# Four tiles in place of one four-bank tile, and a new written order of all work, in a scan followed by a gated feed-forward kernel

## The chip, the cores and the metric

The kernel runs on one core of one Trainium2 chip. The metric is the device time of one execution in microseconds. TensorE is called PE (its weight loads PEld), VectorE DVE, ScalarE ACT, GpSimd POOL and SyncE SP; SP issues nearly all transfers.

## The reference

Inputs are x (4 batches, 8 heads, 768 positions, 32 wide), a (a decay per position), B and C (16 wide), and three weight matrices. Everything is float32. First comes a linear recurrence over the positions, in chunks of 32:

```
L = exp(cum_i - cum_j) * causal;  M = (C B^T) * L
y = M x + (C state) * exp(cum)
state = exp(sum la) * state + sum_j B_j x_j exp(cum_last - cum_j)
```

Then y, as 3072 tokens of 256, goes through a gated layer: `(sigmoid(y @ w_gate) * (y @ w_val)) @ w_out`, with a hidden width of 1536.

## The kernel before

**Work.** The 768 positions are six chunks of 128, numbered 0 to 5. A chunk's scan is a set of small matmuls on 64x64 or 32x128 pieces: `scan` (L494) writes the four-bank PSUM tile pcb and the local states, DVE's `decays` (L458) makes the decays by four scans (L464), `weigh` (L518) multiplies and adds up y with matmuls at L593 and L534. Each chunk gives 512 tokens, a block of the gated layer. Products are made in about float32 by splitting each operand into a high and a low fp32r part and adding three matmuls.

**Blocks 0 to 3** (`gate`, `value`, `proj`). For each f of 0 to 11 the products pg and pv (six matmuls each, L871; block 0 uses whole float32 weights for its first ones, L850, L862, L901) go to one of three PSUM banks. ACT takes the sigmoid of pg (L800), DVE multiplies pv with it (L824, the value gate), ACT and POOL split the result (L828, L830). `proj` then makes the output in two halves, in three steps of four f's each.

**Blocks 4 and 5 together** (`unit`, L1011). Their gate and value products for one weight i are a 2x2 block product, made with seven products in place of eight. A unit has two accumulators x and z, each a bank. Units with i % 3 == 2 (2, 5, 8, 11) take banks 2 and 3 of the tile acc, the others take banks of the pools of three and one. Between the products, `kept` copies a bank (L1042, ACT or DVE) and `summed` adds a bank to a copy (L1050, DVE); `gated` and `hidden` make the sigmoid (L1061, L1064) and the gated product (L1074, L936) and split it (L1088, L936). `paired_proj` (L1098) adds block 4's output into banks 0 and 1 of acc (L1110). `last_proj` makes block 5's output at the end. The unit's third operand, sums of weights, is made on POOL and DVE, stored to DRAM (w_s) and loaded again (s, L964), which may start when block 3's last value product (value3_11) is done.

**Weights.** w0 to w11 are the gate and value weights (even i gate, odd i value, two f's each), w12 to w17 the output weights. After its load each is converted on DVE, ACT, DVE, ACT, POOL (`split_w`, L365 to L385) and, most of them, split (`part_w`, L400, L402).

**Order.** The program writes out each engine's instructions in one fixed order, and the framework puts a semaphore wait wherever an instruction touches a tile that another engine touched. The order is found by a planner (`run`, L215), which acts before the program exists. Each task (`gate1_3`, `decays2`, `w5`) is a chain of steps with an engine, an assumed cost, needs and makes. Over and over it finds the step that could begin first, and takes, among the steps of that engine that could begin within 0.1 us of it, the one whose task has the lowest due time. Due times stand in DUES or, where it has no entry, come from the code at the end: decays2 has 85.0, value1_f has 77 + 2.74 f, weigh5 183, value3_11 206.5. It looks at the 400 tasks of lowest due time only.

Of the kernel before, what the change touches and what calls it, by code (L numbers as in the profile page):

```python
# [8 lines left out]
F32 = mybir.dt.float32  # L9
# [80 lines left out]
def tile_ssd_then_gated_ffn(  # L90
# [39 lines left out]
    ps_cb = ctx.enter_context(tc.tile_pool(name="ps_cb", bufs=1, space=PSUM))  # L130
# [84 lines left out]
    def run():  # L215
# [10 lines left out]
        spare = {"y": [0.0], "cb": [0.0], "cx": [], "cz": [], "o": [0.0] * 4}  # L226

        tasks.sort(key=lambda t: t[:2])
        while tasks:
            ready_ones = []  # L230
            for n, (_, _, (eng, cost, needs, makes, port, buffers, take, give), ready, gen, name) in enumerate(tasks[:400]):
                if any(k not in made for k in needs) or any(m > len(spare[k]) for k, m in buffers.items()):
                    continue
                banks = sum(k == "bank" for k, _ in take)
                some = len(take) - banks
                if some > len(rooms) or any(t is None for t in turns[-3 : len(turns) - 3 + banks]):
                    continue
                ready = max([ready] + turns[-3 : len(turns) - 3 + banks] + [t for t, _ in rooms[:some]])
                for k, m in buffers.items():
                    ready = max([ready] + spare[k][: max(m, 0)])  # L240

                def begin(e):
                    s = max([free[e], ready] + [made[k][0] for k in needs if made[k][1] != e or e == "sp"])
                    return max(s, port_free[0]) if e == "pool" or (e == "dve" and port) else s

                if not isinstance(eng, str):
                    cost, eng = min(zip(cost, eng), key=lambda ce: begin(ce[1]) + ce[0] + SPARE * (ce[1] == "dve"))
                ready_ones.append((begin(eng), eng, n, cost))
# [116 lines left out]
    def split_w(i):  # L365

        yield step("dve", DVE_1, [("raw", i)], port=True)
        raw = raws.pop(i)  # L370
        lw, hw = raw[:, :, :, 0], raw[:, :, :, 1]
        nc.vector.tensor_scalar(
            out=hw.bitcast(F32), in0=hw.bitcast(F32), scalar1=-W_MAX, scalar2=W_MAX, op0=ALU.max, op1=ALU.min
        )
        yield step("act", ACT_SB, [("t", i - 2)])
        t = wk.tile([P, 2, 2 * P], F32, tag="ut", name=f"wt{i}")
        nc.scalar.activation(t, hw.bitcast(F32), AF.Prelu, scale=2.0**-112, alpha=2.0**32)
        yield step("dve", DVE_1, [], [("t", i)], port=True)
        nc.vector.tensor_scalar(
            out=hw, in0=t.bitcast(U32), scalar1=3, scalar2=None, op0=ALU.logical_shift_left  # L380
        )
        yield step("act", ACT_SB, [("raw", i)])
        nc.scalar.activation(lw.bitcast(I32), lw, AF.Copy, scale=2.0**-29)  # L383
        yield step("pool", 1.08, [], [("whole", i)])
        nc.gpsimd.tensor_tensor(out=lw.bitcast(I32), in0=hw.bitcast(I32), in1=lw.bitcast(I32), op=ALU.add)  # L385
        whole[i] = lw.bitcast(F32)
        halves[i] = hw.bitcast(F32), lw.bitcast(F32)

    halves = {}

# [225 lines left out]
    class FirstUnit:  # L616
# [64 lines left out]
        def result(self):  # L681
# [6 lines left out]
            yield step("pe", 0.75, [("xn", b), ("first", 0, b - 1), ("bdec", 0, b)], [("y", 0, b)] + [("y", 0)] * (b == NB - 1), banks=1, y=1)  # L688
# [146 lines left out]
    def needs_of(k, f, j):  # L835
        xs = [("xp", i) for i in range(2)] if k == 0 and not thin(k, f) else [("x", k, i) for i in range(NB)] if k == 0 else [("x", k)]
        return [("whole" if thin(k, f) else "w", f // 2 * 2 + j)] + xs + ([("pv", k, f - 1)] if f else []) + ([("proj", k - 1)] if f > 2 else [])
# [44 lines left out]
    def proj(k, m):  # L882
# [3 lines left out]
        for n, f in enumerate(fs):  # L886
            start, stop = n == 0, n == NF - 1
            if n % 4 == 0:
# [3 lines left out]
                if n == 0:  # L892
                    needs.append(("gv", k))
                yield step(
# [116 lines left out]
    def unit(i):  # L1011
# [5 lines left out]
        if kind == 2:  # L1017
            x, z = (got["acc"][:, n] for n in (2, 3))
# [35 lines left out]
    def gated(j, n):  # L1054
# [3 lines left out]
        if n == 2:  # L1058
            yield step("act", ACT_MM, [("unit", i)], [("sig", j, n)], take=[("g", ("c", i, n))], **drop)
# [3 lines left out]
        yield step("act", ACT_SB, [("c", i, n)], [("sig", j, n)])  # L1063
        nc.scalar.activation(got["c", i, n], got["c", i, n], AF.Sigmoid)  # L1064

    def hidden(j, n):
# [3 lines left out]
        if n == 2:  # L1070
            drop = ({"give": [("bank", ("X", i))]}, {"give": [("bank", ("X", i))]}, {"cx": -1})[i % 3]
            yield step("dve", DVE_MM, [("unit", i), ("sig", j, n)], **drop)
# [3 lines left out]
        else:  # L1076
            eng = yield step(("dve", "pool"), (DVE_SB, POOL_SB), [("c", i, n), ("sig", j, n)], port=True, give=[("g", ("c", i - 1, n))])
# [14 lines left out]
    def accumulators():  # L1092

        yield step("none", 0.0, [("S", NCH - 1)], [("acc",)], cb=1)
        got["acc"] = ps_cb.tile([P, NQ, 512], F32, tag="pcb", name="acc")
        yield step("none", 0.0, cx=-1, cz=-1)

    def paired_proj(j):  # L1098

        for m in range(NK):  # L1100
# [5 lines left out]
            for n in range(2):  # L1106
                hi, lo = (wo[j][:, n, p, ms] for p in range(2))
                hh, hl = (hs[SA, 2 * j + n][:, p] for p in range(2))
                for q, (a, b) in enumerate(((hi, hh), (hi, hl), (lo, hh))):
                    nc.tensor.matmul(  # L1110
                        got["acc"][:, m], a, b, start=(j == 0 and n == 0 and q == 0), stop=(q == 2), skip_group_check=True
                    )

    def paired_out(m):

        yield step("none", 0.0, [("po", SA, m, NF // 2 - 1)])
        yield from turned_out(SA, m, got["acc"][:, m], {}, "act" if m else "sp")
# [99 lines left out]
    def loads_of(c):  # L1217
        block = [("gv", 0)] if c == 2 else []

        def some(key, n, transfer, size, needs, fns):  # L1220
# [3 lines left out]
            **some("a", 2, 2.75, 64, [("y", max(c - 2, 0)), ("a_z",)], lambda: load_a(c)),  # L1224
            **some("bq", 2 * NB, 0.18, 128, [("bt", c - 1)], lambda: load_rows("bq", c, Bm, 1)),
            **some("cq", 2 * NB, 0.18, 128, [("ct", c - 1), ("tp", NB - 1)], lambda: load_rows("cq", c, Cm, 1)),
            f"bn{c}": load(1, 3.2, 4096, [("bdec", c - 2)] + block, [("bn", c)], lambda: load_tokens("bn", c, b4, N, 2)),
# [4 lines left out]
    def initial():  # L1232

        made = [(k, c) for k in ("bt", "ct", "cd", "bdec") for c in (-1, 0)]
        made += [("y", -1), ("t", -2), ("t", -1), ("first", 0, -1), ("inter", 0, -2), ("inter", 0, -1)]
# [14 lines left out]
    for b in range(NB):  # L1250
        named[f"b{b}"] = load(2, 1.5, 1024, [], [("bc", b)], lambda b=b: load_bc(b))
        named[f"x{b}"] = load(1, 0.9, 1024, [], [("xn", b)], lambda b=b: load_x(b))
# [110 lines left out]
```

## Time and profile before

| | us |
|---|---|
| median of 3 runs | 372.23 (371.36 to 374.55) |
| the profiled execution | 372.0 |
| its span, first to last instruction | 370.0 |
| PE busy | 350.0 (95%) |
| POOL, DVE, ACT busy | 248.6, 178.1, 158.5 |
| PE's granted clock, mean | 0.986 of full speed |

Shares are of the span. A matmul counts from its start to a modelled end, and successive matmuls overlap. Times in the rows are from the start of the span.

### The profile page before, as it was taken

How to read it: one execution, taken by the hardware profiler on the slowest of the kernel's cores; microseconds unless marked ns; L12 is line 12 of the kernel's file. 1: busy time of each engine (PE TensorE's matmuls, PEld its weight loads, DVE VectorE, ACT ScalarE, POOL GpSimd, SP SyncE). 2: the span in 40 equal slices, each digit the busy share in tenths (PEclk: the TensorE clock that was granted, in tenths of full speed). 3: DMA queues.
4: the chain of work that ended last, by engine and by line, in shares of the span. 5: the costliest groups of instructions: out<-in, count | busy, mean ns of one | idle time of the engine just before them, and what ended most of it. 6: DMA issues, size and time to landing. Idle time of an engine off the chain costs nothing.

```text
span 370.0 us, 7942 instructions
## 1 busy us (share of the span) xinstructions
PE 350.0 (95%) x3138; PEld 266.1 (72%) x3138; DVE 178.1 (48%) x295; ACT 158.5 (43%) x290; POOL 248.6 (67%) x247
## 2 busy tenths in 40 slices
PE   8989999999979899999999999969998899989896
PEld 3674487567857688888887888758885677757685
DVE  5977686655477554464640536500143425424221
ACT  2667396316733510364412444332075456537200
POOL 3556286684987584489975588749758598947700
PEclk9999999999989999999999999978999999999999
DMA  7987999483934872376344601131354233300013
GB/s 146 191 260 253 218 233 212 90 82 55 177 57 51 124 160 57 105 131 137 103 55 112 113 15 57 47 128 57 89 171 126 70 114 115 113 0 3 0 31 83
DMA packets 100247, 40.15 MB, mean 109 GB/s; under 512 B 88754, under 2 KB 91826, under 8 KB 99570
## 3 DMA queue, kind: packets, MB, share of 16 engines
q1 hardware_dynamic: 97906, 39.39, 47.9%
q8 instruction: 24, 0.39, 0.5%
q10 hardware_dynamic: 2304, 0.26, 0.5%
q14 instruction: 13, 0.11, 0.1%
HBM read 30.00 MB, written 9.63 MB: 107 GB/s over the span
## 4 chain that ended last, share of the span: by engine, by line
PE 76%; DMA 6%; SPq 6%; DVE 5%; issue 4%; ACT 1%; ACTq 1%; DVEq 0%
PE pg L871 15%; PE pv L871 15%; PE po L905 5%; PE acc L1009 5%; PE po L907 5%; PE po L906 5%; PE acc L1110 5%; PE po L901 5%; PE ux L1009 5%; DMA wr<-in_moe_w_gate_dram 4%; PE uz L1009 3%; DVE c L1050 3%; SPq L321 2%; PE pcb L593 2%; DMA wr<-in_moe_w_val_dram 2%
## 5 line engine op out<-in xcount | busy, mean ns | idle before, releaser
L830 POOL TENSOR_TENSOR h<-g,h 128x512 fp32r<-128x512 f32 x38 | 55.7, 1471 | 17.8 <-ACT h L828 17.6
L871 PE MATMUL pg<-xh,w 128*128 128x512 f32 x168 | 59.4, 394 | 2.7 <-DVE g L824 2.3
L871 PE MATMUL pv<-xh,w 128*128 128x512 f32 x168 | 59.6, 395 | 0.0
L824 DVE TENSOR_TENSOR g<-pv,g 128x512 f32<-128x512 f32 x38 | 26.0, 687 | 38.9 <-PE pv L871 35.9
L800 ACT ACTIVATE g<-pg 128x512 f32<-128x512 f32 x48 | 28.8, 600 | 30.7 <-PE pg L871 25.7
L828 ACT CAST h<-g 128x512 fp32r<-128x512 f32 x38 | 23.6, 621 | 39.9 <-DVE g L824 39.6
L871 PEld LDWEIGHTS pg<-xh,w 128*128 128x128 f32 x168 | 31.7, 189 | 10.7 <-DVE g L824 2.8
L936 POOL TENSOR_TENSOR h<-c,h 128x512 fp32r<-128x512 f32 x24 | 30.8, 1298 | 10.0 <-ACT h L1088 10.0
L871 PEld LDWEIGHTS pv<-xh,w 128*128 128x128 f32 x168 | 32.1, 191 | 6.9
L464 DVE TENSOR_TENSOR_SCAN ab<-ab,delta 128x512 f32<-128x512 f32 x20 | 32.7, 1662 | 2.2 <-DMA ab<-a_z 2.2
L871 PE MATMUL pv<-xl,w 128*128 128x512 f32 x84 | 33.2, 395 | 0.0
L871 PE MATMUL pg<-xl,w 128*128 128x512 f32 x84 | 33.0, 392 | 0.0
L905 PE MATMUL po<-h,w 128*128 128x512 f32 x76 | 31.9, 420 | 0.0
L936 POOL TENSOR_TENSOR c<-c,c 128x512 f32<-128x512 f32 x18 | 23.1, 1297 | 11.1 <-DVE c L1050 6.7
L907 PE MATMUL po<-h,w 128*128 128x512 f32 x76 | 30.6, 402 | 0.0
L906 PE MATMUL po<-h,w 128*128 128x512 f32 x76 | 30.5, 402 | 0.0
L402 POOL TENSOR_TENSOR w<-wr,w 128x512 fp32r<-128x512 f32 x18 | 24.1, 1339 | 7.7 <-ACT w L400 7.3
L385 POOL TENSOR_TENSOR wr<-wr 128x512 int32<-128x512 int32 x18 | 19.4, 1084 | 11.5 <-ACT wr L383 10.6
L916 DVE STREAM_TRANSPOSE o<-po 128x256 f32<-128x256 f32 x16 | 6.4, 441 | 42.1 <-PE po L907 31.4
L936 POOL TENSOR_TENSOR sw<-sw 128x128 f32<-128x128 f32 x48 | 21.7, 461 | 0.5
L1110 PE MATMUL acc<-h,w 128*128 128x512 f32 x72 | 18.4, 398 | 3.1 <-DVE c L1050 1.6
L936 POOL TENSOR_TENSOR sp<-sw,sp 128x512 fp32r<-128x512 f32 x12 | 15.7, 1309 | 7.6 <-ACT sp L953 7.6
(179 smaller groups left out, 717.1 us busy)
## 6 DMA issues: line engine op xcount, KB each, us to landing
w_s<-sp SPq DMA_DIRECT2D x12, 512.0 KB
s<-w_s SPq DMA_DIRECT2D x12, 512.0 KB
ab<-a_z SPq DMA_DIRECT2D x10, 512.0 KB
wr<-in_moe_w_val_dram SPq DMA_DIRECT2D x6, 512.0 KB
wr<-in_moe_w_gate_dram SPq DMA_DIRECT2D x6, 512.0 KB
wr<-in_moe_w_out_dram SPq DMA_DIRECT2D x6, 512.0 KB
xn<-in_x_dram SPq DMA_DIRECT2D x5, 512.0 KB
out_dram<-o SPq DMA_DIRECT2D x144, 16.0 KB
```

The costliest lines, as they stand in the source:

```text
L402: engines[eng].tensor_tensor(out=lo, in0=lw, in1=hi.bitcast(F32), op=ALU.subtract)
L464: nc.vector.tensor_tensor_scan(out=t, data0=t, data1=delta.rearrange("p h l -> p (h l)"), initial=0.0, op0=ALU.mult, op1=ALU.add,)
L800: nc.scalar.activation(gs[k, f], pm, AF.Sigmoid)
L824: nc.vector.tensor_tensor(out=g, in0=pm, in1=g, op=ALU.mult)
L830: engines[eng].tensor_tensor(out=hl, in0=g, in1=hh.bitcast(F32), op=ALU.subtract)
L871: nc.tensor.matmul(pm, w[:, part, kt, fs], xx[:, kt], start=(i == 0), stop=(i == 3 * NK - 1))
L905: nc.tensor.matmul(acc, hi, hh, start=start, stop=False)
L906: nc.tensor.matmul(acc, hi, hl, start=False, stop=False)
L907: nc.tensor.matmul(acc, lo, hh, start=False, stop=stop)
L936: engines[eng].tensor_tensor(out=out, in0=in0, in1=in1, op=op)
L1009: nc.tensor.matmul(out, a[i], b[j], start=start and n == 0, stop=n == 2, skip_group_check=True)
L1110: nc.tensor.matmul(got["acc"][:, m], a, b, start=(j == 0 and n == 0 and q == 0), stop=(q == 2), skip_group_check=True)
```

## The change

One: the pool of pcb is closed once the last chunk has been scanned, and a new pool takes its four banks as four tiles acc0 to acc3, where acc was one tile of four banks. Banks and users are the same.

Two: needs that the planner did not know are stated, and names that stood for two things are parted: block 0's x loads make "xb" in place of "xn" (which the loads of later chunks make too), the units' sigmoids make "sigmoid" in place of "sig"; block k's first gate needs the last sigmoid of block k - 1, the second half of a `proj` needs the same step of the first half at its first and last steps, the loads of a and bn need those of the chunk before. The temporary of `split_w`, a ring of two buffers in the order of i, becomes two tiles handed out to whichever split comes.

Three: DUES gets an entry for nearly every task, all new, and the planner looks at all tasks.

Due times that are named below, before and after:

| task | before | after |
|---|---|---|
| w1, w0, w3, w2, w4 | -404, -381, -208, -79, -37 | -1559, -1196, -477, -353, -108 |
| w13, w5, w8, w6, w11 | 79, -100, 2, -45, 121 | -96, -45, 101, 204, 233 |
| w7, w10, w9, w17, w15 | -16, -26, 183, 178, 186 | 264, 367, 528, 554, 870 |
| w14, w12, w16 | 435, 346, 605 | 1128, 1633, 1859 |
| a1_0, a1_1, a2_0, a2_1 | 27, 34, 38.3, 38.3 | -1207, -659, -562, 275 |
| decays2 | 85.0 | -1126.3 |
| value1_0 to value1_5 | 77 to 90.7 | 635, -627, -502, -1159, -1346, -1266 |
| value1_6 to value1_11 | 93.4 to 107.1 | 1809, -1580, -625, 675, -696, -1342 |
| weigh5 | 183 | 26.85 |
| gate3_10, value3_10, value3_11 | 203.8, 203.8, 206.5 | 617, -354, 1046 |
| part7, part9, gate0_11 | 174, -130, -124 | 763, 720, 1125 |
| proj0_0 | 72.3 | -1692 |

```diff
 DUES = {
...
+    "b1": -1341.63, "p": -1823.1, "value0_2": 183.3, "b0": -1784.92, "w1": -1558.96, "w0": -1195.71, "x0": -959.76,
...
+    "out1": -400.25, "w12": 1632.86, "bq1_0": 433.14, "value0_7": -271.37, "w14": 1128.2, "x1_": 1189.86,
+    "value0_4": 560.89, "w16": 1858.63,
 }
...
-    ps_cb = ctx.enter_context(tc.tile_pool(name="ps_cb", bufs=1, space=PSUM))
+    chunk_banks = ctx.enter_context(ExitStack())
+    ps_cb = chunk_banks.enter_context(tc.tile_pool(name="ps_cb", bufs=1, space=PSUM))
...
-            for n, (_, _, (eng, cost, needs, makes, port, buffers, take, give), ready, gen, name) in enumerate(tasks[:400]):
+            for n, (_, _, (eng, cost, needs, makes, port, buffers, take, give), ready, gen, name) in enumerate(tasks):
...
-        yield step("act", ACT_SB, [("t", i - 2)])
-        t = wk.tile([P, 2, 2 * P], F32, tag="ut", name=f"wt{i}")
+        yield step("act", ACT_SB, ut=1)
+        tag = free_ut.pop(0)
+        t = wk.tile([P, 2, 2 * P], F32, tag=tag, name=f"wt{i}", bufs=1)
...
+                if m and n in (0, NF - 4):
+                    needs.append(("po", k, 0, n // 4))
...
-            x, z = (got["acc"][:, n] for n in (2, 3))
+            x, z = got["acc"][2:]
...
-        got["acc"] = ps_cb.tile([P, NQ, 512], F32, tag="pcb", name="acc")
+        chunk_banks.close()
+        banks = chunk_banks.enter_context(tc.tile_pool(name="ps_acc", bufs=1, space=PSUM))
+        got["acc"] = [banks.tile([P, 512], F32, tag=f"acc{n}", name=f"acc{n}") for n in range(4)]
...
-                        got["acc"][:, m], a, b, start=(j == 0 and n == 0 and q == 0), stop=(q == 2), skip_group_check=True
+                        got["acc"][m], a, b, start=(j == 0 and n == 0 and q == 0), stop=(q == 2), skip_group_check=True
...
-        yield from turned_out(SA, m, got["acc"][:, m], {}, "act" if m else "sp")
+        yield from turned_out(SA, m, got["acc"][m], {}, "act" if m else "sp")
```

## Rows read from the trace of the kernel before

**Rows 1.** Busy time by stretch; columns PE, PEld, DVE, ACT, POOL, clock, DMA share, GB/s.

```profile
24.70:100.00 75.30, 74.94 (x559) 48.99 (x559) 48.01 (x82) 43.01 (x74) 49.07 (x44) 1.00 0.84 170
100.00:264.00 164.00, 156.47 (x1830) 127.66 (x1829) 74.57 (x112) 56.48 (x95) 121.67 (x120) 0.97 0.42 89
264.00:348.00 84.00, 77.57 (x327) 59.65 (x326) 33.05 (x50) 43.70 (x79) 61.27 (x57) 1.00 0.27 81
348.00:370.00 22.00, 18.67 (x104) 16.02 (x102) 3.75 (x9) 2.64 (x6) 3.95 (x4) 1.00 0.23 48
...
45.00:62.00 17.00, 16.95 (x74) 13.84 (x75) 13.15 (x24) 15.77 (x29) 13.16 (x12) 1.00 1.04 219
```

**Rows 2.** PE's waits: line, releaser, us in total, times, longest.

```profile
PE pcb L534 <- issue: 5.2, 3, 3.2
PE acc L1009 <- DVE c L1050: 3.1, 6, 1.5
PE pg L871 <- DVE g L824: 2.3, 1, 2.3
PE acc L1110 <- DVE c L1050: 1.6, 2, 0.8
PE acc L1110 <- ACT c L1061: 1.5, 2, 0.7
```

**Rows 3.** Timeline, end of unit 2: start, us, instruction [idle before, releaser].

```profile
283.14 0.97 PE L1009 MATMUL acc<-ops,s 128*128 128x512 f32 x3 [0.84 <-DVE c L1050]
...
284.84 0.69 DVE L1050 TENSOR_TENSOR c<-acc,c 128x512 f32<-128x512 f32 x1 [1.75 <-PE acc L1009]
...
285.58 1.65 PE L1110 MATMUL acc<-h,w 128*128 128x512 f32 x6 [0.78 <-DVE c L1050]
...
287.33 0.60 ACT L1061 ACTIVATE c<-acc 128x512 f32<-128x512 f32 x1 [1.14 <-PE acc L1110]
...
287.98 1.65 PE L1110 MATMUL acc<-h,w 128*128 128x512 f32 x6 [0.75 <-ACT c L1061]
```

**Rows 4.** Timeline, end of unit 11.

```profile
343.23 1.52 PE L1009 MATMUL acc<-ops,s 128*128 128x512 f32 x6
...
344.88 1.29 DVE L1050 TENSOR_TENSOR c<-acc,c 128x512 f32<-128x512 f32 x2 [4.25 <-PE acc L1009]
...
346.23 0.50 PE L1009 MATMUL acc<-ops5h,w 128*128 128x512 f32 x1 [1.48 <-DVE c L1050]
```

**Rows 5.** Timeline of DVE and PE in block 1.

```profile
92.64 1.22 DVE L464 TENSOR_TENSOR_SCAN ab<-ab,delta 128x512 f32<-128x512 f32 x1
...
100.81 6.43 DVE L464 TENSOR_TENSOR_SCAN ab<-ab,delta 128x512 f32<-128x512 f32 x3
107.16 1.26 DVE L824 TENSOR_TENSOR g<-pv,g 128x512 f32<-128x512 f32 x2
...
107.88 0.50 PE L871 MATMUL pg<-xh,w 128*128 128x512 f32 x1 [2.35 <-DVE g L824]
```

**Rows 6.** Busy time and granted clock after two stops of PE.

```profile
108.00:112.00 4.00, 4.00 (x12) 3.08 (x12) 0.42 (x1) 1.67 (x3) 3.86 (x4) 0.60 0.27 45
246.00:252.00 6.00, 5.60 (x19) 4.42 (x20) 0.00 (x0) 2.32 (x4) 3.84 (x4) 0.50 0.02 5
```

**Rows 7.** PE after two stops, and DMA queue and issues of 240 to 247 us.

```profile
123.87 0.27 PE L534 MATMUL pcb<-ct,sn 32*64 32x64 f32 x1 [1.65 <-issue]
...
246.40 0.49 PE L534 MATMUL pcb<-ct,sm 32*64 32x64 f32 x7 [3.21 <-issue]
...
q8 instruction: 1, 0.02, 0.9%
...
s<-w_s SPq DMA_DIRECT2D x2, 512.0 KB
```

**Rows 8.** The first output product, and the last two conversions of weights.

```profile
61.56 10.46 PE L901 MATMUL po<-h,wr 128*128 128x512 f32 x24
...
70.62 2.10 POOL L385 TENSOR_TENSOR wr<-wr 128x512 int32<-128x512 int32 x2 [0.42 <-DVE wr L379]
```

More of the change, by code (lines that the diff above doesn't have):

```diff
@@ L18 @@
 DUES = {
[26 rows of a table removed]
[63 rows of a table added]
+    "parts first": 660.9, "parts rest": 882.75, "proj3_0": -1318.01, "sums10": -891.29, "parts T2": -1661.94,
[23 rows of a table added]
 }
@@ L225, in run @@
         made = {}
-        spare = {"y": [0.0], "cb": [0.0], "cx": [], "cz": [], "o": [0.0] * 4}
+        spare = {"y": [0.0], "cb": [0.0], "cx": [], "cz": [], "o": [0.0] * 4, "ut": [0.0] * 2}
         tasks.sort(key=lambda t: t[:2])
@@ L374, in split_w @@
         )
-        yield step("act", ACT_SB, [("t", i - 2)])
-        t = wk.tile([P, 2, 2 * P], F32, tag="ut", name=f"wt{i}")
+        yield step("act", ACT_SB, ut=1)
+        tag = free_ut.pop(0)
+        t = wk.tile([P, 2, 2 * P], F32, tag=tag, name=f"wt{i}", bufs=1)
         nc.scalar.activation(t, hw.bitcast(F32), AF.Prelu, scale=2.0**-112, alpha=2.0**32)
-        yield step("dve", DVE_1, [], [("t", i)], port=True)
+        yield step("dve", DVE_1, port=True, ut=-1)
         nc.vector.tensor_scalar(
@@ L381, in split_w @@
         )
+        free_ut.append(tag)
         yield step("act", ACT_SB, [("raw", i)])
@@ L389, in tile_ssd_then_gated_ffn @@
     halves = {}
+    free_ut = ["ut0", "ut1"]
     def part_w(i):
@@ L687, in result @@
             weigh(m, self.pcb, self.dec)
-            yield step("pe", 0.75, [("xn", b), ("first", 0, b - 1), ("bdec", 0, b)], [("y", 0, b)] + [("y", 0)] * (b == NB - 1), banks=1, y=1)
+            yield step("pe", 0.75, [("xb", b), ("first", 0, b - 1), ("bdec", 0, b)], [("y", 0, b)] + [("y", 0)] * (b == NB - 1), banks=1, y=1)
             first_y[0] = False
@@ L836, in needs_of @@
         xs = [("xp", i) for i in range(2)] if k == 0 and not thin(k, f) else [("x", k, i) for i in range(NB)] if k == 0 else [("x", k)]
-        return [("whole" if thin(k, f) else "w", f // 2 * 2 + j)] + xs + ([("pv", k, f - 1)] if f else []) + ([("proj", k - 1)] if f > 2 else [])
+        return [("whole" if thin(k, f) else "w", f // 2 * 2 + j)] + xs + ([("pv", k, f - 1)] if f else [("sig", k - 1, NF - 1)] if k else []) + ([("proj", k - 1)] if f > 2 else [])
     def first_half(j):
@@ L1058, in gated @@
         if n == 2:
-            yield step("act", ACT_MM, [("unit", i)], [("sig", j, n)], take=[("g", ("c", i, n))], **drop)
+            yield step("act", ACT_MM, [("unit", i)], [("sigmoid", j, n)], take=[("g", ("c", i, n))], **drop)
             got["c", i, n] = room(("c", i, n))
@@ L1062, in gated @@
             return
-        yield step("act", ACT_SB, [("c", i, n)], [("sig", j, n)])
+        yield step("act", ACT_SB, [("c", i, n)], [("sigmoid", j, n)])
         nc.scalar.activation(got["c", i, n], got["c", i, n], AF.Sigmoid)
@@ L1071, in hidden @@
             drop = ({"give": [("bank", ("X", i))]}, {"give": [("bank", ("X", i))]}, {"cx": -1})[i % 3]
-            yield step("dve", DVE_MM, [("unit", i), ("sig", j, n)], **drop)
+            yield step("dve", DVE_MM, [("unit", i), ("sigmoid", j, n)], **drop)
             g = got["c", i - 1, n]
@@ L1076, in hidden @@
         else:
-            eng = yield step(("dve", "pool"), (DVE_SB, POOL_SB), [("c", i, n), ("sig", j, n)], port=True, give=[("g", ("c", i - 1, n))])
+            eng = yield step(("dve", "pool"), (DVE_SB, POOL_SB), [("c", i, n), ("sigmoid", j, n)], port=True, give=[("g", ("c", i - 1, n))])
             g = got["c", i, n]
@@ L1223, in loads_of @@
         return {
-            **some("a", 2, 2.75, 64, [("y", max(c - 2, 0)), ("a_z",)], lambda: load_a(c)),
+            **some("a", 2, 2.75, 64, [("y", max(c - 2, 0)), ("a_z",)] + [("a", c - 1, i) for i in range(2) if c > 1], lambda: load_a(c)),
             **some("bq", 2 * NB, 0.18, 128, [("bt", c - 1)], lambda: load_rows("bq", c, Bm, 1)),
             **some("cq", 2 * NB, 0.18, 128, [("ct", c - 1), ("tp", NB - 1)], lambda: load_rows("cq", c, Cm, 1)),
-            f"bn{c}": load(1, 3.2, 4096, [("bdec", c - 2)] + block, [("bn", c)], lambda: load_tokens("bn", c, b4, N, 2)),
+            f"bn{c}": load(1, 3.2, 4096, [("bdec", c - 2)] + block + [("bn", c - 1)] * (c > 1), [("bn", c)], lambda: load_tokens("bn", c, b4, N, 2)),
             f"x{c}_": load(1, 3.6, 4096, [("y", c - 1)] + block, [("xn", c)], lambda: load_tokens("xn", c, x4, D, 1)),
@@ L1234, in initial @@
         made = [(k, c) for k in ("bt", "ct", "cd", "bdec") for c in (-1, 0)]
-        made += [("y", -1), ("t", -2), ("t", -1), ("first", 0, -1), ("inter", 0, -2), ("inter", 0, -1)]
+        made += [("y", -1), ("first", 0, -1), ("inter", 0, -2), ("inter", 0, -1)]
         made += [("used", i) for i in (-2, -1)]
@@ L1251, in tile_ssd_then_gated_ffn @@
         named[f"b{b}"] = load(2, 1.5, 1024, [], [("bc", b)], lambda b=b: load_bc(b))
-        named[f"x{b}"] = load(1, 0.9, 1024, [], [("xn", b)], lambda b=b: load_x(b))
+        named[f"x{b}"] = load(1, 0.9, 1024, [], [("xb", b)], lambda b=b: load_x(b))
     for i in range(NW):
```

109 rows, old and new, of the table DUES are left out of this document.

## The prediction

> **What bounds the kernel now.** I read the page's busy shares first, then busy time by stage, then what PE waited for, then the timeline around each wait. PE is the engine to watch: from 24.7 us, where the gated product starts for good, to the end the other engines are busy far less than it is in every stage, and DMA never sets PE's pace [rows 1]. PE's busy time is work that the change does not touch, so what can be won is only the time in which PE stands still or runs at half clock. Between 24.7 and 100 us there is 0.4 us of that, between 100 and 264 us 7.5, between 264 and 348 us 6.4, and 3.3 in the last 22, which is mostly the last outputs going to memory [rows 1]. The view of PE's waits names them: "issue" 5.2 us, value gates of DVE 2.3, and three kinds of wait at the tile acc with 3.1, 1.6 and 1.5, that is 6.2 us in ten waits [rows 2].
>
> **Whose waits the acc waits are.** In the timeline of units 2 and 8 the same chain stands; unit 2's is shown. PE adds the last product of the unit into bank 2 (L1009, 283.14). DVE then reads bank 3 for c (L1050, 284.84), although what it needs was finished three matmuls earlier. PE's output product (L1110), which writes bank 0, starts only when that read is over: 0.78 us of idle, ended by a DVE instruction whose result it does not use. ACT's sigmoid of bank 2 (L1061, 287.33) waits for that L1110 to end, and the second L1110, for bank 1, waits for the sigmoid: 0.75 us [rows 3]. None of these pairs shares a bank; they share only the tile. At the end of unit 11 it is worse: DVE may not begin either of its two reads until PE has finished both products, and PE's last product waits for both reads: 1.48 us [rows 4].
>
> **The sum, part by part.** It is made against the profiled execution, 372.0 us with a span of 370.0; that is 0.2 under the median of the runs shown, so nothing is corrected.
>
> 1. Four tiles in place of one. Nothing is added on any engine: the same matmuls, reads and banks. What goes are waits between banks. In rows 3 both waits go entirely (the operands of L1110 come from ACT and POOL and were ready before). In rows 4 the first read needs only the first of the two products before it, three matmuls earlier or 0.7 us, half of their 1.52; and PE's last product needs only that first read, not the second (1.29 for both), which is another 0.6. So it starts about 1.3 us sooner. Bounds: 0, if every wait were a real operand's, and 6.2, all of rows 2 at acc. I take 5.2, because the rows that I could follow are almost wholly false waits, and leave 1.0 for the real chain of a unit (product, copy, add, product), which shows as soon as no false one hides it. What is late next is that chain, covered by the other unit in flight and by the output products. **-5.2.**
>
> 2. The pool is closed and opened again on the same four banks. The new tiles wait for the last readers of pcb, as acc did. The ring "ut" of two becomes two tiles, and the index order of the splits is given up: the same two buffers. The new names (xb, sigmoid) and needs are used by the planner alone; they issue nothing and wait for nothing on the chip, since every real dependency had its semaphore already. These go together at nothing, in the order they give being part of item 3.
>
> 3. New due times, over all tasks instead of the 400 first. This moves instructions and issues none, but it can move each of the other stops, and make new ones. What there is to win:
> - The stop at 105.5. Three scans of DVE stood in a row before a value gate, 6.43 us for three where a single one took 1.22 at 92.6; PE, waiting for a bank, stood for 2.35 us [rows 5], and then the granted clock was 0.60 in the mean over 4 us [rows 6], which costs 4 x 0.40 = 1.6. Together 4.0. DVE takes the lower due time of what is ready: before, decays2 (85.0) stood ahead of all value1_f from f = 3 on; now it stands behind f = 3, 4, 5, 7 and 11 and ahead of the seven others. The two value products that DVE took up late, at 107.16 [rows 5], are f = 5 and 6, counted from the first of the block, so one of them is protected now. I count half: **-2.0** (bounds 0 and -4.0).
> - The two stops called issue, 1.65 us at 122 and 3.21 us at 243 [rows 7]. Both lie in the runs of 64-column matmuls of weigh. At 243 two 512 KB loads of s fill the DMA engines while PE's queue of instructions gets one packet [rows 7]; then the clock is at 0.50, the 1.2 GHz level, from 246 to 252 [rows 6]; PE works through 5.6 us of that, which costs 2.8. Together 7.7. The s loads may start when value3_11 is done; before, weigh5 came right behind it. Now weigh5 (26.85) is due ahead of gate3_10 and value3_11 (617, 1046) but behind value3_10 (-354), so it escapes only if its operands come one product sooner; they came about when value3_11 began. A third: **-2.6** (bounds 0 and -7.7).
> - New stops elsewhere. The trace of before cannot show them. The lower bound is none, the upper is the rival below (13.5); near is the one at 122, and with 75 us of PE without a gap to lose, I take a little more than that: **+2.6**.
>
> The Trainium skill, "Runtime: NRT & Kernel Launch", section "Instruction fetch mechanics", says that the sequencer fetches the next block of instructions while it runs the current one and that crossing a block is mostly hidden. By it the two stops would not be fetches, no order would move them, the second term would be 0 and the sum 2.6 higher. Rows 7 rather show PE halted with no semaphore to wait for, just while a bulk load fills the engines; no row here names the cause outright.
>
> Sum: 372.0 - 5.2 - 2.0 - 2.6 + 2.6 = 364.8; I say **365**.
>
> **The rivals.**
> - *All stops go.* Units -6.2, DVE -4.0, issue -7.7, none new: 372.0 - 17.9 = 354.1; with two thirds of it, 360. For it: every stop has an owner in the order of work. Against: the runs of small matmuls are five, and each can meet a load.
> - *The waits were real or the order gives the gain back* (no change). If splitting the tile does not part the waits and is worth 1 to 2 us, or one new stop of 5 to 7 us falls in the gapless first 100 us, the time is 368.5 to 375.7. For it: ACT is busy 15.8 of the 17 us from 45 to 62 [rows 1], and part7, part9 and gate0_11 (763, 720, 1125) are now due after most other ACT work there.
> - *The first output product waits for its weight* (slower). proj0_0 starts at 61.56 and its first step needs w12. Before, w12 was sixteenth of the weights; now it is the last but one, due at 1632.86, and the loads of a1 and a2 (-1207 to 275) may pass it too. The last two conversions of weights ended at 70.62 + 2.10 = 72.7 [rows 8]. If w12 takes their place and PE finds nothing else, it stops 11.2 us and then pays 1.6 to 2.8 for the clock, as after the stops above: 13.5 in all, so 372.0 - 5.2 + 13.5 = 380. It decides from the point where w12 is whole after about 68 us: then the loss is 8.9 or more. Against it: a1 ahead of w12 also brings scan1, weigh1 and the first three gates and values of block 1 forward: six products of six matmuls, up to 1.5 us each [rows 4], that could run in that hole.
>
> **How the numbers follow.** A difference of under 1% (368.5 to 375.7) cannot be told from no change here. My forecast's own case, the units' waits gone and the rest about balanced, 360 to 368.5: 0.48. All stops go, under 360: 0.17. No change: 0.20. Slower: 0.15, of which w12's rival is 0.08 and other new stops 0.07. So faster by over 1%: 0.65, same 0.20, slower 0.15. The range leaves out the far half of the second case and half of the slower one: 356 to 377; the likeliest case's own range is 360 to 368.5.
>
> **What would show it.** Right: no PE wait at the acc tiles on a DVE or ACT instruction that reads another bank; PE idle between the first unit and the last under 2 us, not 6; L1110 starting straight behind L1009. Item 3: the scans of DVE apart, with value gates between them, and no gap of 2 us in PE in block 1; weigh5's small matmuls ended before the first s load starts. Wrong: waits of L1009 or L1110 on L1050 of the same length as before; an idle PE or a granted clock of 0.50 between 25 and 100 us, which would say that the new order of loads or of ACT's work costs more than I took; or PE busy time in a stage that changes by more than the clock explains, since I have taken the work itself as fixed.

## The result, and the profile after

The kernel after takes **351.53 us** (350.75 to 353.02, 4 runs) against 371.8 for the kernel before on the same chip, a ratio of 0.9454 (95% interval 0.9386 to 0.9523). The forecast was 365 with a range of 356 to 377: the direction was right, the gain was 20.2 us where 7.2 was said, and the time lies below the range. The profiled execution is 351.77 us, its span 349.7, and the clock is at its full level throughout (mean 1.000).

Busy time by stretch of the kernel after, with the columns of [rows 1]:

```profile
24.70:100.00 75.30, 73.16 (x548) 46.34 (x548) 47.01 (x83) 42.86 (x75) 50.81 (x45) 1.00 0.77 159
100.00:264.00 164.00, 164.00 (x1886) 135.00 (x1885) 75.75 (x121) 59.90 (x104) 119.89 (x122) 1.00 0.46 100
264.00:330.00 66.00, 66.00 (x297) 54.80 (x296) 26.87 (x41) 42.07 (x75) 61.10 (x57) 1.00 0.27 91
330.00:349.70 19.70, 16.12 (x89) 13.69 (x87) 3.85 (x9) 1.49 (x4) 0.61 (x1) 1.00 0.26 54
```

By its matmul rows PE does not stand for one hundredth of a microsecond from 100 to 330 us. Before, it lost 7.5 and 6.4 us in the two middle stretches [rows 1]. PE's waits in the kernel after (line, releaser, us in total, times, longest), where [rows 2] had stood:

```profile
PE warm L206 <- DVE warm_sb L203: 1.1, 1, 1.1
PE pv L936 <- POOL w L467: 0.8, 1, 0.8
...
PE pg L936 <- POOL w L467: 0.2, 1, 0.2
```

No kind of wait of [rows 2] is left; the largest wait behind the start is a new one, at 60.5 us, for a weight that POOL splits. By milestones of the two timelines (first matmul of each), the 20.2 us come from two stages:

| stage | before | after | difference |
|---|---|---|---|
| start of the span to block 1's first product | 86.3 | 89.1 | +2.8 |
| blocks 1 to 3, to the first unit product | 179.4 | 166.5 | -12.9 |
| unit products (312 matmuls of 512 columns with the output products among them) | 81.5 | 70.9 | -10.6 |
| from there to PE's last matmul | 19.5 | 19.6 | +0.1 |

The end of unit 11 in the kernel after, for [rows 3] and [rows 4] (start, us, instruction, idle before and releaser):

```profile
321.91 0.69 DVE L1117 TENSOR_TENSOR c<-acc,c 128x512 f32<-128x512 f32 x1
322.06 0.39 PE L1076 MATMUL ux<-ops5h,w 128*128 128x512 f32 x1
...
322.29 2.88 PE L1179 MATMUL acc<-h,w 128*128 128x512 f32 x12
...
325.01 0.84 PE L1076 MATMUL acc<-ops,s 128*128 128x512 f32 x3
...
325.69 0.39 PE L1076 MATMUL acc<-ops5h,w 128*128 128x512 f32 x1
...
325.89 0.69 DVE L1117 TENSOR_TENSOR c<-acc,c 128x512 f32<-128x512 f32 x1 [3.29 <-PE acc L1076]
```

The output product (L1179) starts at 322.29 while DVE still reads another acc bank until 322.60, and PE's last product (325.69) runs ahead of DVE's read. The scans of chunk 2 and the clock where [rows 5] and [rows 6] stood:

```profile
98.15 2.12 DVE L529 TENSOR_TENSOR_SCAN ab<-ab,delta 128x512 f32<-128x512 f32 x1
100.27 0.69 DVE L889 TENSOR_TENSOR g<-pv,g 128x512 f32<-128x512 f32 x1
100.87 1.57 DVE L529 TENSOR_TENSOR_SCAN ab<-ab,delta 128x512 f32<-128x512 f32 x1
102.98 0.69 DVE L889 TENSOR_TENSOR g<-pv,g 128x512 f32<-128x512 f32 x1 [0.54 <-PE pv L936]
103.59 1.57 DVE L529 TENSOR_TENSOR_SCAN ab<-ab,delta 128x512 f32<-128x512 f32 x1
```

```profile
108.00:112.00 4.00, 4.00 (x78) 3.15 (x76) 1.38 (x2) 1.51 (x4) 1.29 (x1) 1.00 0.89 154
246.00:252.00 6.00, 6.00 (x28) 4.97 (x27) 0.82 (x2) 0.62 (x1) 5.92 (x8) 1.00 0.34 124
```

Between two scans there is now a value gate, and the clock does not fall in this execution. The first output product, the place of the slower rival [rows 8]:

```profile
64.35 10.46 PE L968 MATMUL po<-h,wr 128*128 128x512 f32 x24
```

It runs 24 matmuls without a stop.

### The profile page after: what moved, and what is told of

It reads as the page before. It is cut to its first block, busy times and chain, and to the rows that moved or that the text cites. A ratio compares the mean times of both kernels' runs of the same rounds, so it can differ in the third digit from the quotient of the medians.

```text
span 349.7 us, 7935 instructions
## 1 busy us (share of the span) xinstructions
PE 341.5 (98%) x3140; PEld 263.7 (75%) x3140; DVE 172.1 (49%) x293; ACT 159.2 (46%) x292; POOL 244.4 (70%) x247
## 4 chain that ended last, share of the span: by engine, by line
PE 82%; POOL 0%; issue 0%; ACT 0%; DVE 0%
PE pv L936 15%; PE pg L936 15%; PE ux L1076 6%; PE acc L1076 5%; PE po L972 5%; PE po L968 5%; PE po L974 5%; PE po L973 5%; PE acc L1179 5%; PE uz L1076 5%; PE po L1206 2%; PE pcb L658 2%; PE pcb L643 2%; PE pcb L599 2%; PE po L1207 1%; PE pl L668 1%
## 5 line engine op out<-in xcount | busy, mean ns | idle before, releaser
L895 POOL TENSOR_TENSOR h<-g,h 128x512 fp32r<-128x512 f32 x38 | 51.9, 1369 | 18.9 <-ACT h L893 18.9
L936 PE MATMUL pv<-xh,w 128*128 128x512 f32 x168 | 58.8, 391 | 0.8 <-POOL w L467 0.8
L529 DVE TENSOR_TENSOR_SCAN ab<-ab,delta 128x512 f32<-128x512 f32 x20 | 30.9, 1574 | 1.0 <-DMA ab<-a_z 1.0
L972 PE MATMUL po<-h,w 128*128 128x512 f32 x76 | 30.6, 403 | 0.0
L974 PE MATMUL po<-h,w 128*128 128x512 f32 x76 | 29.6, 389 | 0.0
L973 PE MATMUL po<-h,w 128*128 128x512 f32 x76 | 29.6, 389 | 0.0
L449 POOL TENSOR_TENSOR wr<-wr 128x512 int32<-128x512 int32 x18 | 19.5, 1088 | 11.1 <-ACT wr L447 11.0
L1155 ACT CAST h<-c 128x512 fp32r<-128x512 f32 x24 | 14.7, 623 | 7.7 <-DVE c L1141 5.0
```

The source lines that it names most:

```text
L529: nc.vector.tensor_tensor_scan(out=t, data0=t, data1=delta.rearrange("p h l -> p (h l)"), initial=0.0, op0=ALU.mult, op1=ALU.add,)
L895: engines[eng].tensor_tensor(out=hl, in0=g, in1=hh.bitcast(F32), op=ALU.subtract)
L936: nc.tensor.matmul(pm, w[:, part, kt, fs], xx[:, kt], start=(i == 0), stop=(i == 3 * NK - 1))
L972: nc.tensor.matmul(acc, hi, hh, start=start, stop=False)
L973: nc.tensor.matmul(acc, hi, hl, start=False, stop=False)
L974: nc.tensor.matmul(acc, lo, hh, start=False, stop=stop)
```

## The experiments

**Four tiles alone.** The kernel before with the tile's edit and nothing else; every engine's order is that of before.

```diff
-            x, z = (got["acc"][:, n] for n in (2, 3))
+            x, z = got["acc"][2:]
...
-        got["acc"] = ps_cb.tile([P, NQ, 512], F32, tag="pcb", name="acc")
+        chunk_banks.close()
+        banks = chunk_banks.enter_context(tc.tile_pool(name="ps_acc", bufs=1, space=PSUM))
+        got["acc"] = [banks.tile([P, 512], F32, tag=f"acc{n}", name=f"acc{n}") for n in range(4)]
```

> The kernel before with the four acc tiles alone; every engine's order of work is that of before. Theory U (the weight loads' waits are the true price of the shared tile): the stretch from the first unit product to the last, 81.5 us before, falls to its 312 matmuls x 0.227 us = 70.8, the three other stops stay, total 371.8 - 10.7 = 361. The size that the prediction took: stretch 76.3, total 366.6. Rival W (the waits were for real operands): stretch 81.5, total 372.

Measured: 361.12 us against 371.54, ratio 0.9729 (0.9647 to 0.9811), -10.4; the unit stretch is 71.4 us. What [rows 2] showed of it was 6.2. The view that shows it all is that of the weight loads (PEld) in the unit stretch of the kernel before, in the same columns as [rows 2]:

```profile
PEld acc L1009 <- DVE c L1050: 6.2, 7, 1.9
PEld acc L1110 <- DVE c L1050: 2.4, 2, 1.2
PEld acc L1110 <- ACT c L1061: 2.3, 2, 1.2
PEld acc L1009 <- ACT c L1042: 1.0, 2, 0.6
```

Together 11.9 us (two more kinds have 0.4 and 0.2). With four tiles one line is left:

```profile
PEld acc L1010 <- DVE c L1051: 0.6, 1, 0.6
```

The two views differ because a matmul counts as busy for 0.389 us and the next starts 0.227 after it: at a stop, the modelled end of the last matmul covers the first 0.16 us, and the first matmul behind it counts as busy for 0.50 [rows 4]. Five of the loads' 15 waits have no counterpart at all among the ten of the matmuls. The least time of this stage is 312 matmuls x 0.227 = 70.8, so 81.5 - 70.8 = 10.7 was lost, and that could be read before the change.

**The new order alone.** The kernel after with the tile's edit taken back (the diff above, reversed).

> The kernel after with acc made one tile of four banks again; order, needs and due times are those of after. Theory U: the two parts add up, the unit stretch is back at about 81.5 and the total at 351.5 + 10.7 = 362; PE waits at L1009-like unit products on DVE's summed and ACT's sigmoid. Rival O (the new order of the units took the waits away and the tile split alone does little): stretch 71 to 74, total 352 to 355.

Measured: 361.26 us, ratio 0.9746 (0.9673 to 0.9820); unit stretch 80.6, blocks 1 to 3 166.7. The new order does nothing for the units, and the tile nothing for the blocks: the parts add up.

**The s loads held, by the planner.** The kernel before; the edit gives s0 and s1 one more need.

```diff
-        before = [("gv", PAIR - 1)] if i < 2 else ...
+        before = [("gv", PAIR - 1), ("yw", PAIR + 1)] if i < 2 else ...
```

> The kernel before, with the loads s0 and s1 held until ACT has copied chunk 5's y, so that no bulk load runs during weigh5; PE's order is unchanged to the instruction. Theory B (the prediction's: the bulk load causes the stop called issue): the stop of 3.2 us at 243 and the half clock behind it go, total 371.8 - 6 = 366. Theory I (the stop comes where a run of small matmuls meets PE's own next block of instructions): the stop stays at the same matmul (the second of the eighth group of eight of L534) but is shorter, 1.7 as at 122, because the load only held up the packet; total 370 with the clock's loss, 367.5 if the shorter stop leaves the clock alone.

Measured: 372.14, ratio 1.0018 (0.9977 to 1.0059). It tested nothing: the need changed no engine's order, the program is that of before, instruction by instruction, and SP issued the two loads at 240.59 (240.79 before). It shows what no change looks like, and that the stop stays at the same matmul from run to run (2.88 us at 245.87).

**The s loads held, on the chip.** The same, and the two loads go out on ACT behind its copies of chunk 5's y.

```diff
-        nc.sync.dma_start(sums[i]...
+        (nc.scalar if i < 2 else nc.sync).dma_start(sums[i]...
```

> The kernel before, with s0 and s1 issued by ACT behind its two copies of chunk 5's y, so that they cannot start while weigh5 runs (holding them in the planner alone had moved nothing, since SP takes them as soon as w_s is written). PE's order is that of before to the instruction. Theory I (position in the instruction stream): weigh5 still stops at its 186th matmul, 98 behind the start of a 16 KB block of PE's program, for 1.6 to 2.9 us, and weigh2 as before; total 370 to 372. Theory B (bulk load): no stop at weigh5 and no half clock; total 366.

Measured: 368.25, ratio 0.9899 (0.9823 to 0.9976). The loads start behind the stop, on ACT's queue, and the stop is there without them (timeline, then the clock behind it, columns of [rows 6]):

```profile
246.25 0.34 PE L534 MATMUL pcb<-ct,sm 32*64 32x64 f32 x7 [1.57 <-issue]
...
246.66 0.34 ACTq L964 DMA_DIRECT2D s<-w_s  x1
```

```profile
246.00:252.00 6.00, 5.75 (x31) 4.71 (x32) 0.00 (x0) 2.32 (x4) 4.13 (x4) 1.00 0.50 178
```

So the bulk load does not make this stop. It seems to make it longer: 2.88 to 3.21 in the four runs of this order that were profiled with the loads there (before, four tiles, the planner's hold, and the scans apart below), 1.57 in the one without. The whole time is not the place to read it, since in this run the clock fell behind the stop of weigh2 instead (0.72 over 124 to 130 us) and a stop of 1.34 us stood at 45.9.

**The place in PE's program.** If not the load, what? Over the whole kernel the queue of PE's instructions takes 24 packets and 0.39 MB, 16 KB each; 3138 matmuls and as many weight loads are 262 a packet. I took 256 instructions (128 matmuls with their loads, a float32 matmul counting twice, as in the trace) and counted PE's program, with the instructions that only wait for a semaphore. Between the two stops of before lie 1403 matmuls with their loads and 10 such waits, 2816 instructions, which is 11 x 256: both fall at the same place of a block. Call that place, in every block, a mark. (The expectations give it as 98 matmuls behind a block's start; that figure depends on where the count begins, the distance does not.) The edit moves PE's whole program against the marks by adding small matmuls of nothing at the start; no order and no load changes.

```diff
+    for i in range(23):
+        q = i % 4 * 32
+        nc.tensor.matmul(
+            warm[q : q + 32, :64], warm_sb[:64, q : q + 32], warm_sb[:64, :64], start=True, stop=True, skip_group_check=True
+        )
     eye = const.tile([P, P], F32, name="eye")
```

> The kernel before with 23 small matmuls of nothing ahead of everything on PE, which move every later PE instruction 92 places down the instruction stream (two weight loads and two matmuls each) and change no order and no load. Theory I: the stops at 122 and at 243 both go, with the half clock behind the second, and one new stop of about 1.7 us comes near the end of weigh1, at 83 us, five matmuls from its end; total 371.8 - 1.65 - 3.2 - 2.8 + 1.7 + at most 1 for the added matmuls = 366 to 367. Theory B: the stops stay where the loads are, at 122 and 243, none at 83; total 372 to 373.

Measured: 366.31, ratio 0.9860 (0.9773 to 0.9947). Timeline of PE:

```profile
83.28 0.28 PE L539 MATMUL pcb<-ct,sm 32*64 32x64 f32 x3
86.66 0.48 PE L539 MATMUL pcb<-ct,sm 32*64 32x64 f32 x5 [3.10 <-issue]
...
243.94 0.28 PE L539 MATMUL pcb<-ct,sm 32*64 32x64 f32 x3 [0.99 <-issue]
```

The stop at 122 is gone, and weigh1, which never stopped before, stops with five matmuls to go, where the count had put it. I had missed two things: that stop is 3.10 long, and weigh5 has one of 0.99 left, at its 140th matmul, which is a mark too. That the whole time came out as expected is partly luck: the clock fell at weigh1's stop in place of weigh5's, and the stop behind DVE's three scans was only 0.41 here, 2.35 before. The places of the stops are the evidence, not the time.

**The same shift on the kernel after**, with 35 small matmuls instead of 23.

> The kernel after with 35 small matmuls of nothing ahead of everything on PE: all later PE instructions stand 140 places later in the stream, order and loads are those of after. Theory I: all five weighs now stop, at their 163rd, 175th, 186th, 176th and 174th matmul (98 behind a 16 KB block's start), for 1.7 to 3.2 us each, some with 2 to 3 us of half clock behind them; with up to 1 us for the added matmuls the total is 351.5 + 10 to 17 = 361 to 368. Theory B (after has no stops because no weigh meets a bulk load): none, total 352 to 353.

Measured: 364.41, ratio to before 0.9781 (0.9692 to 0.9870), by the two ratios some 12 us above the kernel after. All five weighs stop, at the five places named:

```profile
86.50 0.33 PE L604 MATMUL pcb<-ct,sn 32*64 32x64 f32 x3 [2.13 <-issue]
136.66 0.21 PE L604 MATMUL pcb<-ct,sm 32*64 32x64 f32 x1 [2.09 <-issue]
185.66 0.34 PE L604 MATMUL pcb<-ct,sm 32*64 32x64 f32 x7 [1.27 <-issue]
208.33 0.27 PE L604 MATMUL pcb<-ct,sm 32*64 32x64 f32 x1 [1.35 <-issue]
236.75 0.27 PE L604 MATMUL pcb<-ct,sm 32*64 32x64 f32 x2 [1.69 <-issue]
```

The new order is the same in both, so what freed the kernel after of these stops is where its weighs happen to lie. Loads of s are no part of it: here they went out at 251.17, long after weigh5's stop. How many of a weigh's 192 matmuls lie ahead of the last mark in it, and the stop there in us:

| kernel | weigh1 | weigh2 | weigh3 | weigh4 | weigh5 |
|---|---|---|---|---|---|
| before | 105, none | 166, 1.65 | 126, none | 143, 0.32 | 185, 3.21 |
| after | 104, none | 116, none | 127, none | 117, none | 115, none |
| before, 23 added | 187, 3.10 | 120, none | 80, none | 97, none | 139, 0.99 |
| after, 35 added | 162, 2.13 | 174, 2.09 | 185, 1.27 | 175, 1.35 | 173, 1.69 |
| put together by hand (below) | 105, none | 120, none | 81, none | 97, none | 119, none |

The short stop of weigh4 is the third of the three that the first line of [rows 2] counts (timeline of the kernel before):

```profile
196.82 0.27 PE L534 MATMUL pcb<-ct,sm 32*64 32x64 f32 x1 [0.32 <-issue]
```

No mark with up to 127 matmuls ahead of it stopped PE; all ten with 139 or more did. The traces also time the packets of PE's instruction queue, one for each mark. At each of the ten stops a packet of 16 KB had ended 1.3 to 1.5 us before PE went on; at the other 15 places of the table the last packet had ended 2.1 us or more before PE came to the mark. So PE goes on about 1.4 us behind a packet's end, and stands where it gets to the mark sooner.

**The scans apart.** The kernel before with the planner's steps written out in its own order, and two steps of DVE moved: the value gates f = 5 and 6 of block 1 go between the three scans of [rows 5].

```diff
-decays2 decays2 decays2 value1_5 value1_6 value1_7
+decays2 value1_5 decays2 value1_6 decays2 value1_7
```

> The kernel before with one change of order: on DVE the value gates f=5 and f=6 of block 1 are put between the three scans of decays2 that stood in a row; every other engine's order is that of before. Theory of the prediction: PE's stop at 107.9 (2.35 us) and the clock's loss behind it (1.6) go: total 371.8 - 4 = 368. Rival (the scan that is left ahead of a value gate is enough, or PE then waits for the scans' own readers): the stop stays over 1 us, total 371 to 372.

Measured: 367.39, ratio 0.9896 (0.9826 to 0.9965), -3.4. DVE, and the clock where it had fallen to 0.60 [rows 6]:

```profile
102.51 1.51 DVE L541 TENSOR_TENSOR_SCAN ab<-ab,delta 128x512 f32<-128x512 f32 x1
104.62 0.69 DVE L901 TENSOR_TENSOR g<-pv,g 128x512 f32<-128x512 f32 x1 [0.60 <-PE pv L948]
105.23 2.21 DVE L541 TENSOR_TENSOR_SCAN ab<-ab,delta 128x512 f32<-128x512 f32 x1
107.37 0.67 DVE L901 TENSOR_TENSOR g<-pv,g 128x512 f32<-128x512 f32 x1
```

```profile
108.00:112.00 4.00, 4.00 (x138) 3.15 (x137) 1.94 (x4) 2.41 (x4) 2.75 (x3) 1.00 0.33 56
```

The stop at 107.9 is gone, and nothing in block 1 takes its place.

How long that stop is hangs on the scans. In the five profiled runs that have the three scans in a row, between the same gates, it is their time less 4.1 us:

| run | three scans | stop |
|---|---|---|
| before | 6.43 | 2.35 |
| four tiles alone | 5.97 | 1.89 |
| s loads on ACT | 5.92 | 1.83 |
| s loads held by the planner | 5.57 | 1.48 |
| 23 matmuls added | 4.50 | 0.41 |

One such scan took 1.20 to 1.23 us at 63 to 67 us of before, where POOL was idle, and 2.11 to 2.25 in this row, where POOL was busy beside it for half of its time or all of it. That POOL's work is the reason was not tested; a faster scan would be another way to shorten the stop.

**All of it by hand.** The kernel before in its own order with the four tiles, the two gates between the scans, and 23 and 10 small matmuls ahead of gate1_0 and gate3_0 to move weigh2 to weigh5 off the marks. No new due times.

```diff
         keep_warm(pm)
+        for i in range({(1, 0, 0): 23, (3, 0, 0): 10}.get((k, f, j), 0)):
+            q = i % 4 * 32
+            nc.tensor.matmul(
+                pm[q : q + 32, :64], eye[:64, q : q + 32], eye[:64, :64], start=True, stop=True, skip_group_check=True
+            )
```

> The kernel before, in its own order and without new due times, with the four acc tiles, the two value gates between the scans, and 23 and 10 small matmuls of nothing ahead of gate1_0 and gate3_0, which put weigh2 and weigh5 elsewhere in the 16 KB blocks. If the three causes are all there is: 371.8 - 10.7 (tiles) - 4.0 (scans) - 7.7 (two stops and the clock) + 0.8 (33 matmuls) = 350.2, no stop of PE over 1 us between block 1 and the last unit. If the new order of after brings something else: 354 to 358.

Measured: **351.78**, ratio 0.9478 (0.9415 to 0.9542): the kernel after's time. Its weigh5 runs at 238.6 with the s loads in flight, and does not stop. PE's largest waits:

```profile
PE pg L954 <- DVE h L898: 1.3, 1, 1.3
PE warm L293 <- DVE warm_sb L290: 1.1, 1, 1.1
PE pl L681 <- POOL bd L547: 0.7, 1, 0.7
```

Within the intervals the three causes are the whole gain; the new order is one way to be rid of two of them, and of the stops in the weighs by chance.

**The corner that the new order left.** The kernel after, its steps written out, with part10's step on POOL and both of part11's moved ahead of POOL's part of split15 and split14; and the kernel after again beside it.

```diff
 ACT:  ... split14
+part11
 ...
-part11
 POOL: ... clip
+part10 part11
 split15
-part10
 split14
-part11
```

> The kernel after in its own order, but part10's step on POOL and part11's on ACT and POOL come before POOL's part of split15 and split14, so that w10 and w11 are whole sooner; PE, DVE and SP keep their order. If PE's two stops at 58.1 and 60.5 us (0.18 and 0.78, both released by POOL's split of a weight) are the only price of that corner: both go, 351.5 - 1.0 = 350.5. Rival: the conversions that are put back hold up the first output product, a stop of 1 us or more after 62, total 351.5 or above.

> The kernel after, unchanged, on the same chip for the comparison: 351.5.

Measured: 351.21 (350.16 to 351.53, 6 runs), ratio 0.9445 (0.9401 to 0.9490), and 352.15 (351.39 to 352.57) for the kernel after, 0.9471 (0.9431 to 0.9512). The intervals overlap, so 0.9 us is what the medians say and no more. The stops of the kernel after's second run, which the other does not have:

```profile
58.89 0.73 PE L936 MATMUL pg<-xh,w 128*128 128x512 f32 x2 [0.19 <-POOL w L467]
...
61.34 0.72 PE L936 MATMUL pv<-xh,w 128*128 128x512 f32 x2 [0.79 <-POOL w L467]
```

## Why the prediction was wrong, in size and in one cause

**Four tiles, -5.2: right cause, wrong price.** Both waits in rows 3 and the last one in rows 4 were false, as said, and went. The failed step is the bound "6.2, all of rows 2 at acc". Rows 2 list PE's matmul rows; the loss was 10.7 and stood in the weight loads, or in a plain count of matmuls. Measured alone: -10.4. The Trainium skill bears on this: in "Perfetto Trace Analysis", section "Tensor Engine Instruction (MATMUL, LD_WEIGHTS)", the end of a TensorE row is an estimate from its size and not an observation, and section "Identifying the Most-Contended Engine" calls matmul busy time a poor measure of headroom for it. This trace agrees: 75.07 us were busy in the unit stretch of before for what takes 70.80 after.

**The pool, the buffers, the names, 0.** Not taken apart. The version by hand closes the pool too, but reaches the same time without the buffers and the names, so these were worth nothing that can be measured.

**The scans, -2.0 of 4.0.** The mechanism was right and the whole term went, not half: all four scans of decays2 have value gates between them. The scans parted alone gave -3.4 (by the interval, 1.3 to 6.5). The failed step is to count the two gates that had been late before, f = 5 and 6: in the kernel after the gates of f = 1 to 4 stand between the four scans, 3 and 4 among those that the prediction itself had listed as due ahead, and DVE was through with the scans before it came to f = 5.

**The two stops called issue, -2.6 of 7.7.** Here the reasoning failed, not only the size. The prediction tied the stop at 243 to the s loads, and so weigh5's luck to its start. With the loads out of the way the stop stayed (1.57), and with the loads in flight a weigh off the marks ran through. The sign that the prediction had named came true, weigh5 ended at 225.4 and the first s load went out at 239.52; but with 35 small matmuls added the same is so (237.1 and 251.17), and weigh5 stops for 1.69. The place in PE's program decides whether there is a stop. The prediction also passed over the third stop of that line of [rows 2], 0.32 in weigh4. Of the rule that the prediction weighed, the Trainium skill's "Runtime: NRT & Kernel Launch", section "Instruction fetch mechanics" (blocks of 16 KiB, 256 instructions, the next one fetched while the current one runs, crossing mostly hidden), the size of a block agrees with the 16 KB packets here. "Mostly hidden" holds for the products, where no crossing stopped PE, and fails in runs of 64-column matmuls, with stops of 0.32 to 3.21 us. That no order would move these stops, as the prediction drew from it, did not hold: both orders and bare shifts moved them. That the program halts for its own next block is my reading of the count, the shifts and the times of the packets; no row names the wait itself.

**New stops elsewhere, +2.6.** The size fits, by luck, since it was taken from the stop at 122, which is of another kind: 0.18 and 0.78 at 58 to 60 us, and block 1 starts at 89.1 and 89.9 in two runs of the kernel after, at 86.3 to 88.0 in five kernels with before's order and an unchanged start (89.4 in the version by hand). What else the start pays was not taken apart.

With 10.4 for the tiles and the next two terms whole, the prediction's own sum is 372.0 - 10.4 - 4.0 - 7.7 + 2.6 = 352.5 against 351.77.

**The rivals.** All stops gone, to which the prediction gave 0.17, was what came, but its 354.1 carried the same 6.2 for the units; with 10.4 it gives 349.9. The waits were not real, so no change fell. The first output product did not wait: [rows 8] has its counterpart at 64.35, without a stop, although w12 was loaded last but one.

## What to carry to other kernels

Price a stall of TensorE by counting matmuls times their spacing, or by the waits of its weight loads; the matmul rows hide a part of every stop. A tile of several banks is waited for as one, so banks with different readers should be tiles of their own. Where a kernel has runs of very short matmuls, look at where the 16 KB blocks of the program fall in them: a few instructions more or less ahead of the run can be worth microseconds, and a change of order can win or lose them by chance.

## What the runs showed of the hardware that was not expected

- PE stopped ten times in 25 runs of 192 short matmuls, each time at the same place of a block of 256 instructions of its program, for 0.32 to 3.21 us, and went on 1.3 to 1.5 us behind the end of a 16 KB packet of its instruction queue.
- The clock does not follow from a stop's length. Its lower level, 1.2 GHz (0.50 in the rows), came in or behind stops of PE of 2.35 and 3.21 us in before, 3.10 with 23 matmuls added, 2.13 and 2.09 with 35 added on after; it did not come after one of 2.94 us at 242.7 in the kernel with the scans apart, of 1.65 at 123.9 in before, nor of 1.57 above. Yet it came after one of 1.79 at 124.3 in the kernel with the loads on ACT, and after one of 1.64 at 122.5 in the run with the planner's hold, which has the program of before. Why, stays open.
- One order's start differs from run to run: block 1 begins at 86.3 and 87.4 us in two runs of one program (before, and the planner's hold), and at 86.6, 87.1 and 88.0 in three kernels whose engines have the same work up to there.
- One scan of DVE of the same size took 1.20 us in one place of before and 2.25 in another.
